# Attention's output projection in program order, its operands two tiles ahead and its input feature first in DRAM

## The chip, the core and the metric

The kernel runs on one core of a Trainium2 chip. A core has a matrix engine (TensorE, PE in the rows), three engines for element-wise work (VectorE or DVE, ScalarE or ACT, GpSimd or POOL), and SyncE (SP), which here does nothing but issue DMAs. Each engine runs its own queue of instructions in order and waits for the others by semaphores. The metric is the device time of one execution in microseconds.

## The reference

x has 2048 tokens (S) of 640 features (D); attention has 32 heads (H) of 20 features and looks back over 256 tokens; the second block is a gated MLP with 864 (FH) features a half, mixed over the tokens by a 2048 x 2048 matrix.

```
qkv = layernorm(x) @ wqkv                    # [S, 3, H, 20]
p   = softmax(q k^T / sqrt(20)), 0 <= query - key < 256
h   = x + (p @ v, heads side by side) @ wo
z   = gelu(layernorm(h) @ w_in)              # halves z1, z2 of 864
out = h + (z1 * (w_sp @ layernorm(z2) + b_sp)) @ w_out
```

## The kernel before, in words

Matrix products of float32 are made from two parts of a rounded type: a high part (a copy) and a low part (operand less high part), and three products. So each operand costs two element-wise operations, the second with two inputs; `split` and `split_o` make them.

The tokens stand in 16 tiles of 128. After the QKV stage come the attention steps: 8 groups of 4 heads, 16 key tiles each, 128 steps of `score_item` (scores and exponentials), with the row maxima of the group after it (`max_item`) made 16 steps ahead and `pv_item` (probabilities times v) 2 steps behind. Each step also issues one or two loads of 20 rows of q or k (`load_stack`, L270) for the group two further on. `pv_item` copies each 256 tokens of four heads from PSUM into a tile `ot` (L398 on ScalarE, L400 on VectorE) and stores it with one DMA (L401) into the DRAM tensor `o_d` [32 heads, 32 rows, 2048 tokens]. Of a head's 32 rows, 20 are the output, row 20 (DH) is the sum of the probabilities, the rest is unused. After the last group, `inverse_sums` loads the sums of 512 tokens (L339), takes the reciprocal on VectorE (L342) and stores it into `r_d` (L343), four times.

Then the projection with `wo`. `proj_early`, a generator that is advanced once a step through the last group, splits wo (L180, L181) and prepares tiles 0 and 1. `load_o` brings a pair of tiles from `o_d` with five DMAs (L134), features and heads on the partitions, and the inverse sums, repeated for four features, from `r_d` (L140). `norm_o` multiplies (L146), `split_o` makes the two parts (L154 or L152, L155), and `proj_o` issues 30 products (`wo_ps`, L89). The loop at L1149 goes over the tiles: it adds x (L1165), stores h to `h_d` (L1166, from ScalarE's queue), normalises over the features (`layernorm`, statistics L73 and L74 on VectorE, L75 and L76 on GpSimd, scaling L79 on VectorE), and has TensorE transpose the result two tiles later (`turn_h`, `ht_ps`, L775), ScalarE copies it out (`ho`, L650) and SP stores it (`hn_d`). Between these stand pieces of `win1_prep`: w_in in sums of blocks and their two parts, for a product by seven in place of eight blocks (`zl`, `wraw`, L644, L650), loaded at L711. The z stage begins with the products `zv` (L835).

What sets the order: from the start up to `ms.close()`, at the end of the attention loop, TensorE, VectorE, ScalarE and SP run their instructions in program order. Behind it, and on GpSimd everywhere, the scheduler of the build chooses the order, and it may move an instruction ahead into the part before, as it does with loads of x and w_in.

Of the kernel before, what the change touches and what calls it, by code (L numbers as in the profile page):

```python
# [34 lines left out]
def block_kernel(ctx, tc, x, wqk, wv, wo, w_in, wsp, bsp, w_out, out):  # L35
# [13 lines left out]
    o_d = dram.tile([H, 32, S], F32, name="o_d")  # L49
# [31 lines left out]

    def gemm(ps, n, lhs, rhs, ks):

        lh, ll = lhs
        rh, rl = rhs
        for k in range(ks):
            for a, b in ((lh, rh), (lh, rl), (ll, rh)):
                for j in range(2):
                    nc.tensor.matmul(ps[:, j, :n], a(k), b(k, j),  # L89
                                     start=(k == 0 and a is lh and b is rh),  # L90
                                     stop=(k == ks - 1 and a is ll))
# [5 lines left out]
    def open_early(pl):  # L97
        mem["t1"] = pl.tile([P, 2 * KF * D], F32R, name="t1")
        mem["m1"] = pl.tile([P, 6 * D + 4 * P], F32, name="m1")
        mem["xh"] = [pl.tile([P, D], F32, name=f"xh{i}") for i in range(2)]  # L100
        mem["ho"] = [pl.tile([P, D], F32, name=f"ho{i}") for i in range(3)]
        mem["wraw"] = pl.tile([P, 2, 2, HF], F32, name="wraw")
# [26 lines left out]
    def load_o(j):  # L129

        t = slice(2 * j * P, (2 * j + 2) * P)
        ot, rs = m1(j % 2 * 2 * D, KD, 2 * P), m1(6 * D + j % 2 * 2 * P, 2 * P)
        for k in range(KD):
            nc.sync.dma_start(ot[:, k], o_d[:, 4 * k:4 * k + 4, t])  # L134
        for i in range(2):
            ots[2 * j + i] = (ot[:, :, i * P:(i + 1) * P], rs[:, i * P:(i + 1) * P])

        def load_rs():
            base = r_d[:, t]
            nc.sync.dma_start(rs, bass.AP(tensor=base.tensor, offset=base.offset, ap=[[S, H], [0, 4], [1, 2 * P]]))  # L140

        return load_rs

    def norm_o(i, eng):
        ot, rs = ots[i]
        eng.tensor_tensor(out=ot, in0=ot, in1=rs[:, None, :].to_broadcast([P, KD, P]), op=OP.mult)  # L146

    def split_o(i, eng):
        ot, _ = ots[i]
        osp = mem["osp2"] if i % 3 == 2 else t1((2 * KD + i % 3 * 2) * D, 2, KD, P)  # L150
        if eng is nc.vector:
            eng.tensor_copy(out=osp[:, 0], in_=ot)  # L152
        else:
            nc.scalar.activation(osp[:, 0], ot, AF.Copy)  # L154
        eng.tensor_tensor(out=osp[:, 1], in0=ot, in1=osp[:, 0].bitcast(F32), op=OP.subtract)  # L155
        ots[i] = osp

# [7 lines left out]
    def proj_early():  # L165
# [10 lines left out]
        for _ in range(4):  # L176
            yield
        for k in range(KD):
            raw = raws_c.pop(f"wo{k}")
            nc.vector.tensor_copy(wo_s[:, 0, k], raw)  # L180
            nc.vector.tensor_tensor(out=wo_s[:, 1, k], in0=raw, in1=wo_s[:, 0, k].bitcast(F32), op=OP.subtract)  # L181
            if k in (1, 3):
                yield
        yield
        rs = load_o(0)
        yield
        yield
        rs()
        yield
        yield  # L190
        load_o(1)()
        yield
        for i in range(2):
            norm_o(i, nc.vector)
            split_o(i, nc.vector)
            yield


    with ExitStack() as ab:
# [132 lines left out]
        def inverse_sums(c):  # L332
            t = tmp3.tile([P, P], F32, tag="inv", bufs=2, name=f"inv{c}")

            def rows(d, step):
                return bass.AP(tensor=d.tensor, offset=d.offset, ap=[[step, H], [P, 4], [1, P]])

            yield
            nc.sync.dma_start(t, rows(o_d[:, DH, c * 512:(c + 1) * 512], 32 * S))  # L339
            yield  # L340
            yield
            nc.vector.reciprocal(out=t, in_=t)  # L342
            nc.sync.dma_start(rows(r_d[:, c * 512:(c + 1) * 512], S), t)  # L343
            yield
# [26 lines left out]
        def pv_item(u):  # L371
# [20 lines left out]
            if kb % 2:  # L392
# [4 lines left out]
                if u >= NU - 5 or j == 0 and u < NU - LEAD:  # L397
                    nc.scalar.activation(ot, src, AF.Copy)  # L398
                else:
                    nc.vector.tensor_copy(out=ot, in_=src)  # L400
                nc.sync.dma_start(o_d[4 * g:4 * g + 4, :, e:e + 256].rearrange("h d t -> (h d) t"), ot)  # L401
            if kb % 4 == 3:
                if g == 7:
                    inverse.append(inverse_sums(c))
# [176 lines left out]
        for s in range(NU + 2):  # L581
# [5 lines left out]
            for hh in range(4):  # L587
# [9 lines left out]
                if hh == 2 + s - NU and s >= NU:  # L597
                    if s == NU:
                        psB.close()
                        psW = pool(psB, "psW", space=PSUM)  # L600
                    pre_ps.append(proj_o(s - NU, psW.tile([P, 2, 512], F32, tag="wo", bufs=3, name=f"wo_ps{s - NU}")))
                if s >= 2:
                    if hh == 1:
                        pv = pv_item(s - 2)
                        next(pv, None)
                    if hh == 3:
                        next(pv, None)
            if u1 == NU:
# [12 lines left out]
        for f in inverse:  # L621
            for _ in f:
                pass


    ms.close()
# [78 lines left out]
    def win1_prep(raw):  # L705
        seven, last = win1
        src = w_in[:, :FH].rearrange("k (h c) -> k h c", h=2)
        for k in range(2):
# [5 lines left out]
            for f in right_blocks(lambda: [s[k] for s in seven], *(raw[:, b, h] for b in range(2) for h in range(2)),  # L714
                                  eng=nc.gpsimd):
# [50 lines left out]
    def turn_h(i):  # L766
        ht = mem["ho"][i % 3]
        if i < NT - 2:
# [99 lines left out]
    def z2_pair(q, i, j, k):  # L868
# [35 lines left out]
        def stat(t, h):  # L904
# [4 lines left out]
            if h:  # L909
                nc.vector.bn_aggr(out=mv[:, 0:2], in_=st)  # L910
                nc.gpsimd.tensor_scalar(out=mv[:, 2:3], in0=mv[:, 1:2], scalar1=EPS, scalar2=None, op0=OP.add)
                nc.gpsimd.tensor_tensor(out=mv[:, 3:4], in0=mv[:, 2:3], in1=half, op=OP.pow)
                nc.gpsimd.tensor_scalar(out=mv[:, 2:3], in0=mv[:, 0:1], scalar1=mv[:, 3:4], scalar2=-1.0,
                                        op0=OP.mult, op1=OP.mult)

        def norm(t):
            mv = stats[t][1]
            nc.scalar.activation(z[t], z[t], AF.Identity, bias=mv[:, 2:3], scale=mv[:, 3:4])
# [231 lines left out]
    for i in range(NT):  # L1150
        if 1 < i + 1 < NT:
            split_o(i + 1, nc.gpsimd)
        if i % 2 == 0 and i + 4 < NT:
            load_o(i // 2 + 2)()
        if i + 2 < NT:
            norm_o(i + 2, nc.vector)
        for n in (2, 3, 4) if i == 0 else (i + 4,) if i + 4 < NT else ():
            load_x2(n)
        run(i - NT)
        ps = pre_ps[i] if i < 2 else proj_o(i, acc_tile(f"wo_ps{i}"))  # L1160
        if i > 1:
            turn_h(i - 2)
        xt = hs.pop(i)
        h3 = xt.rearrange("p (a b) -> p a b", a=2)
        nc.vector.tensor_tensor(out=h3, in0=ps[:, :, :HD], in1=h3, op=OP.add)  # L1165
# [8 lines left out]
    for n in range(len(steps)):  # L1174
        run(n)
        if n < 2:
            turn_h(NT - 2 + n)
        if n == 2:
            open_d()
            w2p = win2_prep(view(fx, 4 * D + 256, FH))  # L1180
        if n > 2:
# [39 lines left out]
```

## Time and profile before

| | us |
|---|---|
| median of 3 runs | 1161.44 (1158.47 to 1166.19) |
| the profiled execution | 1165.89 |
| its span | 1163.7 |
| mean granted TensorE clock | 0.984 |

| engine | busy us | share of the span |
|---|---|---|
| TensorE | 1102.1 | 95% |
| its weight loads | 994.7 | 85% |
| VectorE | 736.8 | 63% |
| ScalarE | 553.9 | 48% |
| GpSimd | 404.8 | 35% |

The table is a mean over stages: QKV to about 248 us, attention from there to about 485, the projection to 582, then the z stage and what follows. In rows of the profile a line number is that of the kernel before, an arrow points from what is read to what is written, and "x30" counts instructions. In the kernel after the change the same code stands some ten lines lower.

### The profile page before, as it was taken

Reading aid. Unit: us, or ns where it says so; the run is one execution under the profiler, and the core shown is the slowest. Engines: PE = TensorE matmul, PEld = TensorE weight load, DVE = VectorE, ACT = ScalarE, POOL = GpSimd, SP = SyncE. Lnnn points to the kernel's source line nnn. Section 1 sums busy time; section 2 is a strip of 40 time slices with the busy share of each in tenths; the row PEclk is TensorE's granted clock in tenths of the full one; section 3 lists DMA queues with packets and bytes.
Section 4 is the critical chain, followed back from the end, with each engine's and each line's share of the span. In section 5 each row is a group of like instructions: output and inputs, shape, how many; then the busy total and the mean of one; then the engine's idle time right before and its main releaser. Section 6 shows DMA issues by size and latency. Waiting matters only on the chain.

```text
span 1163.7 us, 28646 instructions
## 1 busy us (share of the span) xinstructions
PE 1102.1 (95%) x11152; PEld 994.7 (85%) x11152; DVE 736.8 (63%) x1961; ACT 553.9 (48%) x1181; POOL 404.8 (35%) x530
## 2 busy tenths in 40 slices
PE   6999999999999999788999998999999799999998
PEld 6998886667877777588999997999999699999998
DVE  5541213788999986679858468655547874655542
ACT  4334433258998889534257566433336531222110
POOL 3124443456666667446421066000117420000000
PEclk9999999999999999889999999999999999999999
DMA  4222355545555543578736512232341454444332
GB/s 149 78 69 80 136 169 201 184 152 176 184 182 176 179 136 125 164 233 270 245 138 210 167 65 73 67 130 87 119 152 39 157 167 152 142 132 143 93 94 68
DMA packets 79800, 165.35 MB, mean 142 GB/s; under 512 B 10752, under 2 KB 43264, under 8 KB 75776
## 3 DMA queue, kind: packets, MB, share of 16 engines
q1 hardware_dynamic: 77360, 158.28, 42.0%
q10 hardware_dynamic: 2304, 5.24, 1.2%
q8 instruction: 87, 1.43, 0.5%
q14 instruction: 49, 0.40, 0.1%
HBM read 108.83 MB, written 54.66 MB: 140 GB/s over the span
## 4 chain that ended last, share of the span: by engine, by line
PE 62%; ACT 8%; issue 7%; POOL 7%; DVE 6%; DMA 6%; SPq 3%; ACTq 0%; POOLq 0%; DVEq 0%
PE g L992 21%; PE out_ps L1057 8%; ACT pt L363 5%; PE pv L386 4%; PE bank L300 3%; PE bank L361 3%; PE zx L835 2%; POOL sg L486 2%; PE zv L835 2%; PE zb L886 2%; PE zy L835 2%; PE zw L835 1%; PE wo_ps L89 1%; PE qk L467 1%; PE qk L468 1%
## 5 line engine op out<-in xcount | busy, mean ns | idle before, releaser
L363 ACT ACTIVATE pt<-bank 128x384 f32<-128x384 f32 (+2 forms) x512 | 202.5, 484 | 29.4 <-PE bank L361 22.3
L992 PE MATMUL g<-zl,aw 128*128 128x432 f32 x768 | 174.4, 363 | 8.8 <-ACT zl L650 8.3
L650 ACT ACTIVATE aw<-fx 128x512 fp32r<-128x512 f32 (+2 forms) x160 | 92.9, 595 | 187.3 <-PE g L992 122.3
L310 DVE CUSTOM_DVE_ANT_0 junk<-bank,strip 128x288 bf16<-128x288 f32 x392 | 156.2, 454 | 15.2 <-PE bank L300 13.8
L992 PEld LDWEIGHTS g<-zl,aw 128*128 128x128 f32 x768 | 145.4, 190 | 17.3 <-ACT zl L650 10.5
L992 PE MATMUL g<-ze,aw 128*128 128x432 f32 x576 | 136.2, 366 | 4.6 <-ACT aw L650 4.5
L386 PE MATMUL pv<-pt,v_sb 128*32 128x192 f32 (+3 forms) x1984 | 130.9, 326 | 10.1 <-DVE ot L400 5.0
L644 DVE TENSOR_TENSOR aw<-fx,aw 128x512 fp32r<-128x512 f32 (+2 forms) x152 | 111.9, 746 | 37.0 <-ACT aw L650 36.3
L992 PEld LDWEIGHTS g<-ze,aw 128*128 128x128 f32 x576 | 109.8, 192 | 10.3 <-ACT aw L650 5.2
L361 PE MATMUL bank<-slot 123*32 123x288 bf16 (+7 forms) x1536 | 110.0, 280 | 2.4 <-issue 1.1
L365 POOL TENSOR_SCALAR_AFFINE_SELECT pt<-pt 128x512 f32<-128x512 f32 x128 | 81.9, 640 | 70.6 <-ACT pt L363 69.3
L1057 PE MATMUL out_ps<-wout,y_sp 128*128 128x320 f32 (+1 forms) x630 | 96.2, 309 | 0.4 <-ACT y_sp L122 0.4
L886 PE MATMUL zb<-win,aw 128*128 128x432 f32 x480 | 95.3, 359 | 0.0
L1057 PEld LDWEIGHTS out_ps<-wout,y_sp 128*128 128x128 f32 (+1 forms) x630 | 94.1, 188 | 1.2 <-ACT y_sp L122 0.7
L886 PEld LDWEIGHTS zb<-win,aw 128*128 128x128 f32 x480 | 89.9, 187 | 4.7
L300 PE MATMUL bank<-slot 120*32 120x288 bf16 (+6 forms) x1280 | 92.2, 277 | 0.9 <-issue 0.8
L483 DVE TENSOR_TENSOR rest<-qk,sg 128x512 f32<-128x512 f32 x40 | 27.7, 692 | 89.5 <-ACT sg L481 89.5
L386 PEld LDWEIGHTS pv<-pt,v_sb 128*32 128x32 f32 x1984 | 61.9, 111 | 17.8 <-issue 14.3
L361 PEld LDWEIGHTS <-slot 123*32 123x32 bf16 x1728 | 60.3, 98 | 17.1 <-issue 8.3
L486 POOL TENSOR_TENSOR sg<-rest,sg 128x512 bf16<-128x512 f32 x40 | 46.5, 1164 | 75.1 <-ACT sg L485 73.2
L368 POOL TENSOR_SCALAR_AFFINE_SELECT pt<-pt 128x512 f32<-128x512 f32 x112 | 71.6, 639 | 0.0
L644 DVE TENSOR_TENSOR row<-g,row 128x432 f32<-128x432 f32 x80 | 48.2, 604 | 36.1 <-PE g L992 32.7
(192 smaller groups left out, 2221.1 us busy)
## 6 DMA issues: line engine op xcount, KB each, us to landing
slot<-qk_d SPq DMA_DIRECT2D x144, 160.0 KB
fx<-wsp_in SPq DMA_DIRECT2D x32, 512.0 KB
qk_d<-sg SPq DMA_DIRECT2D x40, 384.0 KB
fx<-hn_d SPq DMA_DIRECT2D x32, 320.0 KB
o_d<-ot SPq DMA_DIRECT2D x64, 128.0 KB
xb<-qk_d SPq DMA_DIRECT2D x48, 160.0 KB
z_d<-row SPq DMA_DIRECT2D x16, 432.0 KB
g_d<-row SPq DMA_DIRECT2D x16, 432.0 KB
```

Source lines behind the costliest of these rows:

```text
L300: nc.tensor.matmul(ps[32 * j:32 * j + 32, o:o + w], one(st, 120, 0, hh, q0, 32), k, start=True, stop=True, tile_position=(0, 32 * j))
L310: nc.vector.tensor_tensor_reduce(out=junk[:, :n], in0=ps[:, :n], in1=keep, scale=1.0, scalar=NEG, op0=OP.add, op1=OP.max, accum_out=m_cols ...
L361: nc.tensor.matmul(ps[32 * i:32 * i + 32, b + o:b + o + w], one(st, 123, 1, hh, k0, 32), q, start=True, stop=True, tile_position=(0, 32 * i))
L363: nc.scalar.activation(pt[:, hh, :n], ps[:, :n], AF.Exp, scale=SCALE)
L365: nc.gpsimd.affine_select(out=pt[:, :, :P], in_=pt[:, :, :P], pattern=[[0, 4], [1, P]], base=0, channel_multiplier=-1, compare_op=OP.is_ge ...
L386: nc.tensor.matmul(ps[32 * hh:32 * hh + 32, a - 512 * c:b - 512 * c], v_sb[:, kb, v0:v0 + 32], pt[:, hh, a - kb * P:b - kb * P], start=fir ...
L644: (eng or nc.vector).tensor_tensor(out=out, in0=a, in1=b, op=op)
L650: nc.scalar.activation(out, a, AF.Copy)
L835: nc.tensor.matmul(ps, a[x], b[:, y], start=start and m + x + y == 0, stop=stop and m == n - 1 and x == 1, skip_group_check=True)
L886: nc.tensor.matmul(b[0][:, :HF], a[t][:, x, kk], win2[0][:, y, kk, h * HF:(h + 1) * HF], start=kk + x + y == 0, stop=kk == KD - 1 and x == 1)
L992: nc.tensor.matmul(ps, w[m][:, x, k], zc[k][m][:, y], start=start and k + x + y == 0, stop=stop and k == 3 and x == 1, skip_group_check=True)
L1057: nc.tensor.matmul(ps[j][:, :HD], src[:w, a, k, :], e1["wout"][:w, b, k, j * HD:(j + 1) * HD], start=(k == 0 and a + b == 0), stop=(k == K ...
```

## The change

- `o_d` becomes [32 rows, 32 heads, tokens]. The store of `ot` writes it with an address pattern whose outer count is the 4 heads, and one load brings a pair of tiles (L145 after). The rows of wo are put in the order that goes with it. The load of the repeated inverse sums has the repetition by 4 outermost.
- VectorE makes all multiplications, low parts and sums of blocks of w_in in this stage; GpSimd keeps three small operations of the statistics a tile. ScalarE does the scaling of the normalisation (`scaled`, L90 after) in VectorE's place.
- A tile's multiplication and split are issued two tiles ahead of its projection, in place of one.
- The inverse sums are made in five pieces (256, 256 and three of 512 tokens) with buffers of their own.
- Program order lasts to step 2 of the z stage, on four engines. h is stored from SP's queue, no longer from ScalarE's.
- The split of wo goes one block a step and starts one step earlier; ScalarE makes the last copy of `ot` only, VectorE the three before it.

```diff
-    o_d = dram.tile([H, 32, S], F32, name="o_d")
+    o_d = dram.tile([32, H, S], F32, name="o_d")
...
+    def scaled(dst, src, mv):
+        nc.scalar.activation(dst, src, AF.Identity, bias=mv[:, 2:3], scale=mv[:, 3:4])
...
-        for k in range(KD):
-            nc.sync.dma_start(ot[:, k], o_d[:, 4 * k:4 * k + 4, t])
+        base = o_d[:, :, t]
+        nc.sync.dma_start(ot, bass.AP(tensor=base.tensor, offset=base.offset, ap=[[S, P], [P * S, KD], [1, 2 * P]]))
...
-            nc.sync.dma_start(rs, bass.AP(tensor=base.tensor, offset=base.offset, ap=[[S, H], [0, 4], [1, 2 * P]]))
+            nc.sync.dma_start(rs, bass.AP(tensor=base.tensor, offset=base.offset, ap=[[0, 4], [S, H], [1, 2 * P]]))
...
-        eng.tensor_tensor(out=ot, in0=ot, in1=rs[:, None, :].to_broadcast([P, KD, P]), op=OP.mult)
+        nc.vector.tensor_tensor(out=ot, in0=ot, in1=rs[:, None, :].to_broadcast([P, KD, P]), op=OP.mult)
...
-                if u >= NU - 5 or j == 0 and u < NU - LEAD:
+                if u >= NU - 2 or j == 0 and u < NU - LEAD:
                     nc.scalar.activation(ot, src, AF.Copy)
                 else:
                     nc.vector.tensor_copy(out=ot, in_=src)
-                nc.sync.dma_start(o_d[4 * g:4 * g + 4, :, e:e + 256].rearrange("h d t -> (h d) t"), ot)
-            if kb % 4 == 3:
-                if g == 7:
-                    inverse.append(inverse_sums(c))
+                base = o_d[:, 4 * g:4 * g + 4, e:e + 256]
+                nc.sync.dma_start(bass.AP(tensor=base.tensor, offset=base.offset,
+                                          ap=[[S, 4], [H * S, 32], [1, 256]]), ot)
+            if g == 7 and (kb % 4 == 3 or kb == 1):
+                n = 256 if kb < 4 else 512
+                inverse.append(inverse_sums((kb + 1) * P - n, n))
...
-            for f in right_blocks(lambda: [s[k] for s in seven], *(raw[:, b, h] for b in range(2) for h in range(2)),
-                                  eng=nc.gpsimd):
+            for f in right_blocks(lambda: [s[k] for s in seven], *(raw[:, b, h] for b in range(2) for h in range(2))):
...
-    for i in range(NT):
-        if 1 < i + 1 < NT:
-            split_o(i + 1, nc.gpsimd)
-        if i % 2 == 0 and i + 4 < NT:
-            load_o(i // 2 + 2)()
-        if i + 2 < NT:
-            norm_o(i + 2, nc.vector)
-        for n in (2, 3, 4) if i == 0 else (i + 4,) if i + 4 < NT else ():
-            load_x2(n)
-        run(i - NT)
-        ps = pre_ps[i] if i < 2 else proj_o(i, acc_tile(f"wo_ps{i}"))
-        if i > 1:
-            turn_h(i - 2)
-        xt = hs.pop(i)
-        h3 = xt.rearrange("p (a b) -> p a b", a=2)
-        nc.vector.tensor_tensor(out=h3, in0=ps[:, :, :HD], in1=h3, op=OP.add)
-        nc.scalar.dma_start(h_d[i], xt)
-        layernorm(hn(i), xt, D, f"c{i}")
-        next(w1, None)
-        if i % 2:
+    for i in range(1, NT + 1):
+        if i < NT:
+            for f in inverse:
+                next(f, None)
+                if i == 2:
+                    next(f, None)
+        if i == 1:
+            split_o(2)()
+        if 1 < i < NT:
+            pre_ps.append(proj_o(i, acc_tile(f"wo_ps{i}")))
+        if i > 1:
+            add_h(i - 1)
+        if i + 2 < NT:
+            norm_o(i + 2)
+            lo = split_o(i + 2)
+        if i == 1:
+            add_h(0)
+        if i < NT:
+            run(i - NT)
+        bn_h(i - 1)
+        if i + 2 < NT:
+            lo()
+        if i == 1:
+            load_o(2)()
+        if i % 2 and i < NT - 5:
+            load_o(i // 2 + 3)()
+        for n in (2, 3, 4) if i == 1 else (i + 3,) if i + 3 < NT else ():
+            load_x2(n)
+        next(w1, None)
+        scaled(hn(i - 1), hs.pop(i - 1), stat_h.pop(i - 1)[1])
+        if i > 1:
+            turn_h(i - 2)
+        if i % 3 == 1:
             next(w1, None)
```

`add_h` adds x and issues the store of h, `bn_h` makes the statistics, and `run` the pieces of the z stage's preparation.

What the diff does to the queues is seen in their order. First TensorE around tiles 6 to 8 of the projection. Before:

```order
L89 MATMUL wo_ps_10335<-t_9342 128x320 x13
L775 MATMUL ht_ps_10302<-ident,m_9343 128x128 x5
L89 MATMUL wo_ps_10335<-t_9342 128x320 x17
L775 MATMUL ht_ps_10366<-ident,m_9343 128x128 x5
L89 MATMUL wo_ps_10390<-t_9342 128x320 x30
L89 MATMUL wo_ps_10450<-t_9342,osp_10018 128x320 x28
L775 MATMUL ht_ps_10421<-ident,m_9343 128x128 x5
L89 MATMUL wo_ps_10450<-t_9342,osp_10018 128x320 x2
```

After:

```order
L784 MATMUL ht_ps_10290<-ident,m_9343 128x128 x5
L99 MATMUL wo_ps_10298<-t_9342 128x320 x30
L784 MATMUL ht_ps_10348<-ident,m_9343 128x128 x5
L99 MATMUL wo_ps_10356<-t_9342 128x320 x30
L784 MATMUL ht_ps_10405<-ident,m_9343 128x128 x5
L99 MATMUL wo_ps_10415<-t_9342,osp_10008 128x320 x30
L784 MATMUL ht_ps_10461<-ident,m_9343 128x128 x5
```

Before, the scheduler put a tile's transposes (`ht_ps`) inside a projection (`wo_ps`) or left them out between two; now one set stands behind each projection.

Next VectorE where attention ends and wo is split; `ot_1_0` and its like are the copies of the last group's output, `CAST` and the subtraction behind it split one block of wo. Before:

```order
L180 CAST t_9342<-m_9343 128x640
L181 TENSOR_TENSOR t_9342<-m_9343,t_9342 128x640
L180 CAST t_9342<-m_9343 128x640
L181 TENSOR_TENSOR t_9342<-m_9343,t_9342 128x640
L400 COPY ot_1_0_9624<-pv_1_9481 128x256
L180 CAST t_9342<-wraw 128x640
L181 TENSOR_TENSOR t_9342<-wraw,t_9342 128x640
L342 RECIPROCAL inv_9524<-inv_9524 128x128
L400 COPY ot_1_1_9699<-pv_1_9481 128x256
L400 COPY ot_2_0_9767<-pv_2_9656 128x256
```

After:

```order
L412 COPY ot_0_1_9522<-pv_0_9401 128x256
L191 CAST t_9342<-m_9343 128x640
L192 TENSOR_TENSOR t_9342<-m_9343,t_9342 128x640
L191 CAST t_9342<-m_9343 128x640
L192 TENSOR_TENSOR t_9342<-m_9343,t_9342 128x640
L412 COPY ot_1_0_9625<-pv_1_9483 128x256
L191 CAST t_9342<-m_9343 128x640
L192 TENSOR_TENSOR t_9342<-m_9343,t_9342 128x640
L354 RECIPROCAL inv_9347<-inv_9347 128x64
L191 CAST t_9342<-wraw 128x640
L192 TENSOR_TENSOR t_9342<-wraw,t_9342 128x640
L412 COPY ot_1_1_9697<-pv_1_9483 128x256
```

The splits now stand between the copies, and the reciprocals, each of 256 tokens, ahead of the copy `ot_1_1`.

Third, ScalarE and SP at the start of the projection's loop after the change; `zl` from `wraw` is the first high part of a block of w_in, L90 the scaling, `L721` the load of w_in. ScalarE:

```order
L165 ACTIVATE osp_10008<-m_9343 128x640
L165 ACTIVATE t_9342<-m_9343 128x640
L90 ACTIVATE m_9343<-xh_9344,mvc_10043 128x640
L165 ACTIVATE t_9342<-m_9343 128x640
L660 ACTIVATE zl_10012<-wraw 128x432
L90 ACTIVATE m_9343<-xh_9345,mvc_10097 128x640
L660 ACTIVATE ho_9348<-ht_ps_10108 128x640
```

SP:

```order
L1159 DMA h_d<-xh_9344 128x640
L145 DMA m_9343<-o_d 128x5x256
L151 DMA m_9343<-r_d 128x1x256
L145 DMA m_9343<-o_d 128x5x256
L151 DMA m_9343<-r_d 128x1x256
L138 DMA xh_10005<-x_in 128x640
L138 DMA xh_10006<-x_in 128x640
L138 DMA xh_10007<-x_in 128x640
L721 DMA wraw<-w_in_in 128x864 x2
```

On ScalarE the piece of w_in stands ahead of the scaling of tile 1 (`xh_9345`), and on SP its load stands behind the first store of h and the loads of two pairs of tiles and three tiles of x; before the change, the scaling was VectorE's and did not stand behind a piece of w_in on ScalarE.

More of the change, by code (lines that the diff above doesn't have):

```diff
@@ L100, in open_early @@
         mem["xh"] = [pl.tile([P, D], F32, name=f"xh{i}") for i in range(2)]
+        mem["inv"] = [pl.tile([P, P], F32, name=f"inv{i}") for i in range(2)]
         mem["ho"] = [pl.tile([P, D], F32, name=f"ho{i}") for i in range(3)]
@@ L175, in proj_early @@
             load_x2(i)
-        for _ in range(4):
+        for _ in range(3):
             yield
@@ L342, in inverse_sums @@
             nc.vector.reciprocal(out=t, in_=t)
-            nc.sync.dma_start(rows(r_d[:, c * 512:(c + 1) * 512], S), t)
+            nc.sync.dma_start(rows(r_d[:, t0:t0 + n], S), t)
             yield
@@ L607, in block_kernel @@
                         next(pv, None)
+                if hh == 2 + s - NU and s >= NU:
+                    if s == NU:
+                        psB.close()
+                        psW = pool(psB, "psW", space=PSUM)
+                    pre_ps.append(proj_o(s - NU, psW.tile([P, 2, 512], F32, tag="wo", bufs=3, name=f"wo_ps{s - NU}")))
             if u1 == NU:
```

85 lines of the change are left out of this document (45 added, 40 removed).

## The prediction

> **What bounds the kernel now.** I read the busy time by stretches first, then the chain of waits, then TensorE's own timeline and waits around the projection. The stretches (columns: length, then busy time of TensorE, its weight loads, VectorE, ScalarE and GpSimd, the granted TensorE clock, the DMA share and GB/s) show which stage is not full:
>
> ```profile
> core 0: us, PE busy (x) PEld busy (x) DVE busy (x) ACT busy (x) POOL busy (x), PEclk, DMA share, GB/s
> 466.00:488.00 22.00, 13.73 (x261) 9.60 (x258) 10.70 (x16) 12.78 (x36) 11.37 (x17) 0.83 0.57 182
> 488.00:582.00 94.00, 85.28 (x562) 82.67 (x562) 79.78 (x131) 30.70 (x54) 49.25 (x52) 0.93 0.73 238
> 582.00:740.00 158.00, 153.27 (x769) 144.84 (x768) 109.38 (x185) 95.01 (x172) 50.75 (x51) 0.98 0.35 120
> ```
>
> TensorE is nearly full, but in the projection (488 to 582) it is busy 85 of 94 us at a clock of 0.93, and in the seam before it 14 of 22 us at 0.83. The chain of waits at the end of that stage shows its pace when nothing is late:
>
> ```profile
> 567.85 4.39 PE wo_ps L89 x30
> 572.25 0.55 PE ht_ps L775 x5
> 572.79 4.40 PE wo_ps L89 x30
> 577.20 0.55 PE ht_ps L775 x5
> ```
>
> A tile takes 4.40 us of projection and 0.55 us of transposes: 4.95 us. TensorE's timeline (start, length, work, in brackets the idle time and who ended it) shows where it was slower:
>
> ```profile
> 471.19 1.08 PE L386 MATMUL pv<-pt,v_sb 128*32 128x256 f32 x8 [5.00 <-DVE ot L400]
> 487.69 5.93 PE L89 MATMUL wo_ps<-t 128*128 128x320 f32 x30 [2.22 <-DVE t L152]
> 509.98 0.74 PE L775 MATMUL ht_ps<-ident,m 128*128 128x128 f32 x5 [1.95 <-DVE m L79]
> 512.27 7.16 PE L89 MATMUL wo_ps<-t 128*128 128x320 f32 x30 [1.55 <-DVE xh L1165]
> 538.23 5.88 PE L89 MATMUL wo_ps<-t,osp 128*128 128x320 f32 x28 [2.92 <-DVE mvc L74]
> 577.50 4.64 PE L89 MATMUL wo_ps<-t 128*128 128x320 f32 x30
> 582.44 1.43 PE L835 MATMUL zv<-zl,aw 128*128 128x432 f32 x6
> 514.00:517.00 3.00, 3.00 (x13) 3.00 (x13) 2.97 (x5) 2.10 (x4) 2.41 (x4) 0.50 0.97 332
> ```
>
> After each wait the next projection is longer too: 5.93, 7.16 and 5.88 us (the last with 28 of 30 products) against 4.64, because the granted clock falls (0.50 in the stretch after the waits at 510 and 512). VectorE ended all these waits.
>
> From the first projection at 487.69 to the first product of the z stage at 582.44 are 94.75 us, and sixteen projections with fifteen transposes at full pace are 16 x 4.40 + 15 x 0.55 = 78.65 (this stretch holds 14 of the transposes now, 15 with the change). So at most 16.1 us can be saved there, 16.6 with the transposes that leave the z stage.
>
> **The change part by part.** *TensorE's order.* Before, transposes stand inside a projection and wait for a normalised tile; now projection and transposes alternate, the normalised tile being due one tile earlier than its transposes. Nothing is added on TensorE. If no operand is late this gives the 16.6 us.
>
> *VectorE and GpSimd.* These rows show durations next to each other and alone:
>
> ```profile
> 488.32 1.55 DVE L146 TENSOR_TENSOR m<-m 128x640 f32<-128x640 f32 x2
> 546.76 2.92 DVE L146 TENSOR_TENSOR m<-m 128x640 f32<-128x640 f32 x2
> 546.74 2.26 POOL L155 TENSOR_TENSOR osp<-m,osp 128x640 fp32r<-128x640 f32 x1
> L146 DVE TENSOR_TENSOR m<-m 128x640 f32<-128x640 f32 x16 | 15.4, 995 | 6.6 <-DMA m<-o_d 3.5 <-DMA hn_d<-ho 1.7 <-DMA r_d<-inv 1.4
> L79 DVE TENSOR_SCALAR m<-xh,mvc 128x640 f32<-128x640 f32 x15 | 12.4, 824 | 5.3 <-POOL mvc L76 5.3
> 487.58 0.82 DVE L155 TENSOR_TENSOR t<-m,t 128x640 fp32r<-128x640 f32 x1
> L644 DVE TENSOR_TENSOR wraw<-wraw 128x432 f32<-128x432 f32 x4 | 2.4, 598 | 0.0
> L154 ACT ACTIVATE t<-m 128x640 fp32r<-128x640 f32 x9 | 6.6, 730 | 11.5 <-DMA m<-o_d 8.8 <-PE wo_ps L89 2.7
> ```
>
> Alone, two of the multiplications by the inverse sums take 1.55 us; beside GpSimd's subtraction they take 2.92. VectorE now gets fourteen subtractions of GpSimd's (14 x 0.82 = 11.5) and eight pieces of win1 (8 x 0.60 = 4.8), loses the scaling to ScalarE (12.4) and the slow-down of the multiplications (16 x (0.995 - 0.775) = 3.5). From 79.8 us busy that makes about 80.2; the other two-input operations that shared time with GpSimd should give back a few us more, and I take 77: 4.8 us a tile, hidden behind TensorE's 4.95 with little to spare. ScalarE's 30.7 us grow by 15 scalings at about the 0.73 us of its other 128x640 operation to 42 of 80: hidden. If the cover is gone, an overrun of VectorE goes straight into the pace (a rival below).
>
> *The seam.* Before, TensorE waits 5.0 us for a copy that stands on VectorE behind four pairs of splits of wo. With the change the first split stands ahead of one copy, where it waits for wo to land, and the first inverse sums stand ahead of another. I expect two waits of about 2 and 3 us in place of the one, so no gain; bounds for the first projection are 3 us earlier (neither waits) and 3 us later (both are as long as the one now).
>
> *A new wait.* In the new program order ScalarE's second piece of win1 stands ahead of the scaling of tile 1, and it waits for a load of w_in that SP issues behind the first store of h, two pairs of attention output and three tiles of x. In the trace that load left SP at 478.57, ahead of them all. Its row, that of the first addition to h, and the sizes:
>
> ```profile
> 478.57 0.44 SPq L711 DMA_DIRECT2D wraw<-w_in_in  x1
> 494.24 0.75 DVE L1165 TENSOR_TENSOR xh<-wo_ps,xh 128x640 f32<-128x640 f32 x1
> h_d<-xh ACTq DMA_DIRECT2D x15, 320.0 KB
> m<-o_d SPq DMA_DIRECT2D x35, 128.0 KB
> m<-r_d SPq DMA_DIRECT2D x8, 128.0 KB
> xh<-x_in SPq DMA_DIRECT2D x11, 320.0 KB
> wraw<-w_in_in SPq DMA_DIRECT2D x3, 432.0 KB
> ```
>
> One h_d, two pairs of 5 x 128 + 128 KB, three x and two blocks of w_in (one into fx, and the one waited for) are 3680 KB or 3.8 MB, at the 332 GB/s of the full stretch above some 11 us. The store of h waits for the first addition, which came 6.6 us after the first projection and now stands behind another multiplication, a split and the pieces of the inverse sums: about 10 us, an estimate. So w_in lands near 22 us, ScalarE's piece and the scaling follow, and the transposes of tile 1 can start near 24; TensorE, after four projections of 4.64 and one set of transposes, would be there at 19. I take 4.9 us of waiting (0 if SP gets through sooner, 8 if the loads go at the stage's mean of 238 GB/s) and 1.8 us for the clock after it (0 to 2.5, from 7.16 against 4.64).
>
> *The loads and stores.* One load for a pair in place of five saves issues on SP, which bounds nothing. The stores of the attention output now go to an address pattern whose outer count is 4 instead of 128. How many of the 16 engines a transfer uses can be read from its small closing packets. An isolated store (432 to 436 us) and a stretch with nothing but the 20-row loads of q and k (182 to 184 us):
>
> ```profile
> DMA packets 146, 0.16 MB, mean 39 GB/s; under 512 B 16, under 2 KB 144, under 8 KB 144
> q1 hardware_dynamic: 144, 0.13, 9.8%
> DMA packets 93, 0.51 MB, mean 254 GB/s; under 512 B 31, under 2 KB 31, under 8 KB 31
> ```
>
> The store has 128 rows and 16 closing packets; the loads have 62 rows of 8 KB with 31 closing packets, ten for twenty rows. So the shape sets the engines, and an outer count of 4 may well mean four. The store takes 0.098 x 16 x 4 = 6.3 us of engine time, 0.39 on each of sixteen, 1.6 on each of four: later by 1.2 us, of which in the middle of attention nobody takes notice as long as those four engines keep up. I put it at 0 there, from the slack of half a group that the loads have, and keep the upper end for the rival. *The Trainium skill, "DMA: Bandwidth & Descriptors", section "Why a DMA increments its semaphore by 16 and not by 1", says that a transfer runs on the largest number of engines up to 16 that divides the outermost count of both patterns, and always on the lowest-numbered ones. By that rule the loads' ten agree with the trace, and the stores would be on four that all loads use too; by it the second rival has the better chance, and the sum would be its time.*
>
> **The sum.** 1165.9 us (the profiled execution: span 1163.7 and 2.2 around it) - 16.6 + 4.9 + 1.8 = 1156.0. The profiled execution lies 4.5 us above the median of the runs shown (1161.44), so the forecast is 1151.5. With the bounds together, not all at one end, 1145 to 1158.
>
> **The rivals.** *The new wait is not there.* w_in is in time, for example because the loads pass SP early; all 16.6 us come: 1161.4 - 16.6 = 1144.8, 1144 with a somewhat earlier seam. For it speaks that DMA is at 0.73 in this stage; against it, that SP's order puts everything ahead of that load.
>
> *Four engines carry the stores and fill up (slower).* Price from these rows:
>
> ```profile
> L401 SPq DMA_DIRECT2D o_d<-ot x64: 319/410/1570, 257.9 to 497.8; - x64
> 181.00:184.00 3.00, 3.00 (x15) 2.41 (x14) 0.69 (x1) 1.23 (x2) 0.67 (x2) 1.00 0.62 257
> q1 hardware_dynamic: 2296, 5.48, 57.5%
> slot<-qk_d SPq DMA_DIRECT2D x23, 160.0 KB
> ```
>
> 64 stores in 239.9 us make 30.4 us for a group of eight. A load of 160 KB keeps its ten engines for 0.64 us at 257 GB/s; in the stretch 310 to 340 all 26 loads (these 23 and 3 into another buffer) and 8 stores have 57.5% of 16 x 30 us = 276, so less 8 x 6.3 a load costs 226 / 26 / 10 = 0.87. With 24 loads and 8 stores at 1.57, four engines need 27.9 us a group at the first price and 33.4 at the second, against 30.4. Above 0.74 us a load they decide: at 0.87 each of six groups is 3.0 us longer, 18 us, and the five stores on the way to the inverse sums add 1.2 each: 1151.5 + 24 = 1175. For it speak the closing packets; against it, that a long packet in a mixed stretch may only overlap another.
>
> *VectorE becomes the bound.* In program order it can't fill a wait with later work, and its 4.8 us a tile are uneven, since preparation of win1 and of the z stage falls on a few tiles. If a tile costs 0.6 us more than TensorE's pace, 16 x 0.6 = 9.6 are given back: 1161.
>
> **How the numbers follow.** A measurement of this kernel can tell about 1% from no change: below 1149.8 is faster, above 1173.1 slower. Chances: forecast 0.42 (four tenths of it below 1149.8), no new wait 0.26 (nearly all faster), four engines 0.22 (two thirds slower), VectorE 0.10 (half slower, as an uneven pace may cost more than worked out). That gives faster 0.44, same 0.36, slower 0.20. The likeliest case's own range is 1145 to 1158; to leave out no more than two in ten the range reaches to 1141 on the side of the first rival and 1172 into the second.
>
> **What would show it.** Right: projections of 4.4 with transposes of 0.55 between them without a break from the fourth tile on, the first product of the z stage 84 to 88 us after the first projection, GpSimd nearly empty there, VectorE's multiplications at 0.75 to 0.8 us, and one gap ahead of the transposes of tile 1 that ScalarE or the load of w_in ended. Wrong: attention longer than from 257.9 to 497.8 by its stores, SP waiting on transfers of m_d or q and k, 32 rows for one closing packet in an isolated store (four engines), or many short gaps that VectorE ended. The stages after the z stage should not move.

## The result and the profile after

The changed kernel takes 1179.31 us (1177.71 to 1183.03, 4 runs) against 1159.95 for the kernel before on the same chip: a ratio of 1.0161, 95% interval 1.0131 to 1.0192. It is slower by 19 us where 10 us less were forecast. The profiled execution is 1183.0 us with a span of 1181.3.

The same stretches as before the change (length, busy time of TensorE, weight loads, VectorE, ScalarE and GpSimd, clock, DMA share, GB/s), and with them the stretch from the first projection to the first product of the z stage:

```profile
466.00:488.00 22.00, 19.24 (x481) 13.28 (x477) 13.96 (x34) 19.91 (x55) 18.56 (x26) 1.00 0.48 151
488.00:582.00 94.00, 75.60 (x603) 72.23 (x591) 57.66 (x103) 36.23 (x67) 25.06 (x44) 0.85 0.68 225
582.00:740.00 158.00, 154.76 (x826) 147.64 (x825) 113.90 (x201) 98.27 (x176) 52.42 (x57) 1.00 0.43 149
506.40:601.20 94.80, 85.00 (x574) 83.52 (x572) 66.10 (x125) 40.64 (x65) 24.45 (x45) 0.92 0.73 245
```

The first row is still full of attention: everything has moved later. TensorE's timeline shows by how much, and what became of the projection:

```profile
505.57 0.87 PE L398 MATMUL pv<-pt,v_sb 128*32 128x192 f32 x8 [6.34 <-DVE ot L412]
506.37 7.08 PE L99 MATMUL wo_ps<-t 128*128 128x320 f32 x30
537.00 1.33 PE L784 MATMUL ht_ps<-ident,m 128*128 128x128 f32 x5 [9.15 <-ACT m L90]
537.98 6.67 PE L99 MATMUL wo_ps<-t 128*128 128x320 f32 x30
549.89 4.64 PE L99 MATMUL wo_ps<-t 128*128 128x320 f32 x30
554.84 4.65 PE L99 MATMUL wo_ps<-t 128*128 128x320 f32 x30
601.21 1.43 PE L844 MATMUL zv<-zl,aw 128*128 128x432 f32 x6
605.23 1.45 PE L844 MATMUL zx<-zl,aw 128*128 128x432 f32 x6 [2.58 <-ACT ho L660]
```

The first projection starts at 506.37 in place of 487.69, 18.7 us later. From there to the first product of the z stage (`zv`) it takes 94.84 us, as before (94.75): the pace between is the predicted 4.95 us a tile (549.89 to 554.84), but a slow first projection (7.08 us), one wait of 9.15 us and the slow projection behind it (6.67 us) eat the gain. Behind it 1181.3 - 601.2 = 580.1 us remain, before 581.3. So the loss is all ahead of the projection. What SP and TensorE waited for between 250 and 480 us (total, times, longest), SP and TensorE before, then SP and TensorE after, and the stores of `ot` after:

```profile
SPq L327 <- DMA m_d<-m: 19.5, 14, 3.4
...
PE bank L361 <- DMA slot<-m_d: 0.7, 1, 0.7
...
SPq L338 <- DMA m_d<-m: 40.6, 15, 5.1
...
PE bank L373 <- DMA slot<-m_d: 12.2, 4, 4.7
PE bank L373 <- DMA xb<-m_d: 3.9, 2, 2.2
...
L414 SPq DMA_DIRECT2D o_d<-ot x64: 512/553/630, 260.5 to 514.4; - x64
```

SP waits twice as long for its store of the row maxima (`m_d`) before it loads them again, and TensorE, which waited 0.7 us for those loads before, waits 16.1 us for them. The stores stretch over 253.9 us (before 239.9), 32.2 us for a group of eight in place of 30.4. The first store starts 2.6 us later than before (260.5 for 257.9), behind a stage that the change leaves alone, and the runs below have it anywhere from 257.9 to 262.4; so some 16 of the 18.7 us arise between it and the first projection. An isolated store, 463 to 467 us (busy share of the engines in 40 slices of 0.1 us, then the packets):

```profile
DMA  0000000023131223228223232000000000000000
DMA packets 133, 0.15 MB, mean 37 GB/s; under 512 B 4, under 2 KB 132, under 8 KB 132
```

and the slices of the one before the change, whose packets the prediction shows (432 to 436 us):

```profile
DMA  0000000000003999500000000000000000200600
```

It now has 4 closing packets (those under 512 B) to its 128 rows, where it had 16, and lasts 1.8 us at a fifth to a quarter of the engines, where it took 0.5 at nearly all.

### The profile page after: what moved, and what is told of

It is laid out like the page before. It is cut to its first block, busy times and chain, and to the rows that moved or that the text cites. A ratio compares the mean times of both kernels' runs of the same rounds, so it can differ in the third digit from the quotient of the medians.

```text
span 1181.3 us, 28599 instructions
## 1 busy us (share of the span) xinstructions
PE 1106.7 (94%) x11152; PEld 998.9 (85%) x11152; DVE 732.2 (62%) x1970; ACT 566.5 (48%) x1194; POOL 380.8 (32%) x524
## 4 chain that ended last, share of the span: by engine, by line
PE 40%; DVE 6%; DMA 5%; POOL 4%; ACT 3%; issue 2%; SPq 0%; DVEq 0%; POOLq 0%; ACTq 0%
PE g L996 20%; PE out_ps L1061 8%; PE zx L844 2%; PE zv L844 2%; PE zb L895 2%; PE zy L844 2%; PE zw L844 1%; DMA m<-r_d 1%; PE wo_ps L99 1%; DVE zl L654 1%; PE yt_ps L1050 1%; POOL row L654 1%; ACT row L90 1%; DVE aw L654 1%; DMA h_d<-xh 1%
## 5 line engine op out<-in xcount | busy, mean ns | idle before, releaser
L660 ACT ACTIVATE aw<-fx 128x512 fp32r<-128x512 f32 (+3 forms) x160 | 93.0, 595 | 172.3 <-PE g L996 113.7
L398 PE MATMUL pv<-pt,v_sb 128*32 128x192 f32 (+3 forms) x1984 | 134.9, 332 | 15.5 <-DVE ot L412 10.1
L654 DVE TENSOR_TENSOR aw<-fx,aw 128x512 fp32r<-128x512 f32 (+3 forms) x152 | 108.5, 724 | 35.2 <-ACT aw L660 34.3
L373 PE MATMUL bank<-slot 123*32 123x288 bf16 (+8 forms) x1536 | 111.6, 281 | 0.5 <-ACT pt L375 0.2
L377 POOL TENSOR_SCALAR_AFFINE_SELECT pt<-pt 128x512 f32<-128x512 f32 x128 | 82.6, 645 | 81.0 <-ACT pt L375 78.8
L311 PE MATMUL bank<-slot 120*32 120x288 bf16 (+5 forms) x1280 | 92.5, 277 | 0.2
L373 PEld LDWEIGHTS <-slot 123*32 123x32 bf16 x1728 | 62.9, 100 | 25.9 <-issue 17.3
L380 POOL TENSOR_SCALAR_AFFINE_SELECT pt<-pt 128x512 f32<-128x512 f32 x112 | 73.9, 660 | 0.0
```

What stands on the lines that cost most here:

```text
L311: nc.tensor.matmul(ps[32 * j:32 * j + 32, o:o + w], one(st, 120, 0, hh, q0, 32), k, start=True, stop=True, tile_position=(0, 32 * j))
L373: nc.tensor.matmul(ps[32 * i:32 * i + 32, b + o:b + o + w], one(st, 123, 1, hh, k0, 32), q, start=True, stop=True, tile_position=(0, 32 * i))
L377: nc.gpsimd.affine_select(out=pt[:, :, :P], in_=pt[:, :, :P], pattern=[[0, 4], [1, P]], base=0, channel_multiplier=-1, compare_op=OP.is_ge ...
L398: nc.tensor.matmul(ps[32 * hh:32 * hh + 32, a - 512 * c:b - 512 * c], v_sb[:, kb, v0:v0 + 32], pt[:, hh, a - kb * P:b - kb * P], start=fir ...
L654: (eng or nc.vector).tensor_tensor(out=out, in0=a, in1=b, op=op)
L660: nc.scalar.activation(out, a, AF.Copy)
```

## The experiments

Theory A, the prediction's second rival: an outer count of 4 puts the store on four engines, which the loads of q and k use as well; the transfers of `m_d` queue behind both. Rivals: B, the new addresses make the stores slow; C, the store's longer issue on SP (0.55 us for 0.41); D, the program order around the end of attention.

**1. Only the pattern (e1_outer4).** In the kernel before:

```diff
-                nc.sync.dma_start(o_d[4 * g:4 * g + 4, :, e:e + 256].rearrange("h d t -> (h d) t"), ot)
+                base = o_d[4 * g:4 * g + 4, :, e:e + 256]
+                nc.sync.dma_start(bass.AP(tensor=base.tensor, offset=base.offset,
+                                          ap=[[32 * S, 4], [S, 32], [1, 256]]), ot)
```

> The kernel before, with one edit: the store of ot is written with an address pattern of outer count 4 (4 x 32 x 256). Addresses, bytes and the number of transfers are those of before. Theory A (an outer count of 4 puts the store on four engines, which the loads of q and k use too, and the transfers of m_d queue behind both): SP waits for m_d for some 40 us in attention as in the changed kernel (20 before), the 64 stores stretch over 252 us or more (240 before), 1160 + 12 to 16 = 1172 to 1176 us. Theory B (the new addresses, a head's rows 256 KB apart, make the store slow): nothing moves, 1158 to 1163. Theory C (only the store's longer issue on SP counts, 0.55 for 0.41 us): 64 x 0.14 = 9 us at most, 1160 to 1169, and SP's waits for m_d stay near 20 us.

1161.90 us, ratio 0.9992 (0.9972 to 1.0012). It tested nothing: with these strides the two outer counts are one count of 128 rows, and so the build issued it. An isolated store of this run, 433 to 437 us, has 16 closing packets:

```profile
DMA packets 146, 0.16 MB, mean 39 GB/s; under 512 B 16, under 2 KB 144, under 8 KB 144
```

**2. The layout of before in the changed kernel (e2_layout).** `o_d` is [heads, rows, tokens] again, with all that hangs on it:

```diff
-    o_d = dram.tile([32, H, S], F32, name="o_d")
+    o_d = dram.tile([H, 32, S], F32, name="o_d")
...
-                                          ap=[[S, 4], [H * S, 32], [1, 256]]), ot)
+                nc.sync.dma_start(o_d[4 * g:4 * g + 4, :, e:e + 256].rearrange("h d t -> (h d) t"), ot)
...
-            nc.sync.dma_start(rs, bass.AP(tensor=base.tensor, offset=base.offset, ap=[[0, 4], [S, H], [1, 2 * P]]))
+            nc.sync.dma_start(rs, bass.AP(tensor=base.tensor, offset=base.offset, ap=[[S, H], [0, 4], [1, 2 * P]]))
```

> The changed kernel with the DRAM layout of before: stores of 128 rows, five loads a pair, inverse sums repeated inside, rows of wo as before. Program order, split of work and two tiles ahead stay. Theory A: SP's waits for m_d fall from 40.6 to about 20 us, the 64 stores to about 240 us, the first projection comes 13 to 16 us earlier, the wait ahead of the transposes of tile 1 shrinks by about 2 us: 1159 to 1165. Rival (the slow-down is of the order, VectorE behind waits in the last steps): the first projection gains at most 5 us, 1172 to 1178.

1166.18 us, ratio 1.0032 (1.0011 to 1.0053): of the 19 us of loss some 4 are left. SP's waits for m_d, the stores, and TensorE at the projection:

```profile
SPq L338 <- DMA m_d<-m: 15.6, 13, 2.4
...
L413 SPq DMA_DIRECT2D o_d<-ot x64: 319/410/1201, 258.9 to 494.8; - x64
...
487.05 6.76 PE L99 MATMUL wo_ps<-t 128*128 128x320 f32 x30
515.74 1.33 PE L782 MATMUL ht_ps<-ident,m 128*128 128x128 f32 x5 [7.51 <-ACT m L90]
```

The first projection comes 19.3 us earlier, where it was before the change: D falls. But what is left of the change gains nothing either, which the next runs are about.

**3. The load of w_in ahead of the loop (e3_win),** and **4. with the layout of before (e4_both):**

```diff
     w1 = win1_prep(mem["wraw"])
+    next(w1)
...
-        next(w1, None)
+        if i > 1:
+            next(w1, None)
         scaled(hn(i - 1), hs.pop(i - 1), stat_h.pop(i - 1)[1])
```

> The changed kernel with the first load of w_in issued ahead of the loop over tiles, so ahead of the first store of h, the loads of two pairs and three tiles of x. Theory: the wait of 9.15 us ahead of the transposes of tile 1 was for this load alone; it goes, with the 2 us of low clock behind it: 1167 to 1171. Rival: the attention output of tile 4 is as late (VectorE waited for its inverse sums until 527), so that a wait of 2 to 5 us stays and the gain is 4 to 8 us: 1171 to 1175.

> Both edits together, the layout of before and the early load of w_in. If the two costs are the whole loss and independent: 1179 - 16 - 10 = 1150 to 1155, 0.5 to 0.9% below before, with 80 to 84 us from the first projection to the first product of the z stage. If they share a cause (both are DMA in the same stage), less than the sum: 1156 to 1162.

1178.60 us, ratio 1.0134 (1.0090 to 1.0178), and 1164.98 us, ratio 1.0014 (0.9988 to 1.0039). Both gain less than expected. TensorE in the first, then VectorE and TensorE in the second:

```profile
527.35 1.33 PE L784 MATMUL ht_ps<-ident,m 128*128 128x128 f32 x5 [4.49 <-ACT m L90]
...
503.67 0.82 DVE L157 TENSOR_TENSOR m<-m 128x640 f32<-128x640 f32 x1 [8.04 <-DMA m<-o_d]
508.33 1.33 PE L782 MATMUL ht_ps<-ident,m 128*128 128x128 f32 x5 [4.78 <-ACT m L90]
```

The wait ahead of tile 1's transposes only falls from 9.15 to 4.49 us, and with the layout of before from 7.51 to 4.78: now VectorE's multiplication of tile 4 waits at the head of VectorE's queue, 7.77 us for its inverse sums in run 3 and 8.04 for its load in run 4, and tile 1's statistics stand behind it. The rival of run 3 had that wait, but not so small a gain.

**5. The layout alone, in the kernel before (e5_layout_alone):** the first edit of run 2 the other way, with the five loads, the scheduler and all else as before.

> The kernel before with the DRAM layout of the change alone: o_d feature first, stores of 4 x 32 x 256, rows of wo to go with it, the repetition of the inverse sums outermost; five loads a pair, scheduler's order and everything else as before. (In the first run of this kind the pattern of outer count 4 had been merged to 128 rows, with 16 closing packets, so it tested nothing; here the strides can't be merged.) Theory A (four engines): an isolated store has 4 closing packets and takes about 1.8 us, SP's waits for m_d rise from 20 to some 40 us, the first projection comes 11 to 16 us later: 1172 to 1180. Rival (the loss comes from program order in the last steps): 1160 to 1165.

1181.83 us, ratio 1.0154 (1.0125 to 1.0183), SP's waits for m_d, the stores, and the packets of one finished store and part of the next (461 to 465 us):

```profile
SPq L327 <- DMA m_d<-m: 42.1, 15, 4.5
...
L402 SPq DMA_DIRECT2D o_d<-ot x64: 517/552/978, 262.4 to 516.1; - x64
...
DMA packets 186, 0.20 MB, mean 50 GB/s; under 512 B 4, under 2 KB 185, under 8 KB 185
```

The layout alone, its stores and its loads together, makes the whole loss; run 12 takes the stores by themselves.

**6 and 9. More issues on SP (e6_sp_issue, e9_sp_24).** The kernel of run 2 with a small extra store behind each store of ot, and behind 24 of the 64:

```diff
+                if (2 * c + j) % 3 == 0:          # run 9 only
+                    nc.sync.dma_start(e_d[8 * g + 2 * c + j], ot[:16, :64])
```

> The changed kernel with the layout of before, and one small extra store (16 rows of 256 B, to a scratch tensor) behind each store of ot, so that SP issues 64 more DMAs of some 0.3 us (more issue time than the 0.14 us by which the store of the change took longer), while the data on each engine hardly grows. Theory A: as without them, 1164 to 1170, SP's waits for m_d below 25 us. Rival (the store's longer issue on SP made the loss): 1175 or more, with loads of q and k issued later.

> As the run with 64 extra small stores, but with 24 of them: at the 0.43 us median that one took on SP that is 10 us more for SP in attention, about what the longer issue of the change's stores costs (64 x 0.14 = 9 us). Theory A (the waits for m_d behind the four engines made the loss, the issue time little of it): within 4 us of the run with the layout of before alone, 1164 to 1170. Rival (SP has no spare time, so that 10 us of issue cost as much): 1173 to 1178.

1182.57 us, ratio 1.0172 (1.0134 to 1.0210), and 1170.31 us, ratio 1.0052 (1.0014 to 1.0090). SP's and TensorE's waits for m_d and the small stores in the first, SP's waits in the second:

```profile
SPq L339 <- DMA m_d<-m: 13.3, 10, 3.1
...
PE bank L374 <- DMA slot<-m_d: 7.9, 4, 5.8
PE bank L374 <- DMA xb<-m_d: 5.4, 2, 2.9
...
L415 SPq DMA_DIRECT2D e_d<-ot x64: 311/427/1641, 260.5 to 510.0; - x64
...
SPq L339 <- DMA m_d<-m: 23.0, 15, 3.0
```

Run 6 went against A's expectation. 64 extra issues, 27 us at their median and more in all, cost 16 us against run 2. SP does not wait longer for m_d, but TensorE now waits 13.3 us for those loads, and none in run 2: a busy SP can bring them late too. Run 9 has the dose that fits C, 24 x 0.43 = 10 us: the first projection came at 489.7 in place of 487.05, and the intervals of runs 2 and 9 overlap. So, as an estimate, the longer issue explains some 3 of the 19 us. Whether SP's 21 us of added waiting for m_d are the rest, run 10 asks.

**7. The loads earlier (e7_early)** and **8. the last transposes too (e8_best).** On the kernel of run 4, in `proj_early` behind `norm_o(2)`, and for run 8 in the loop:

```diff
+        src = w_in[:, :FH].rearrange("k (h c) -> k h c", h=2)
+        for b in range(2):
+            nc.sync.dma_start(mem["wraw"][:, b], src[2 * b * P:(2 * b + 1) * P])
+        load_o(2)()
...
+        if i == NT:                               # run 8 only
+            turn_h(i - 2)
         scaled(hn(i - 1), hs.pop(i - 1), stat_h.pop(i - 1)[1])
-        if i > 1:
+        if 1 < i < NT:
             turn_h(i - 2)
```

The loads of x for tiles 2 to 4 stand ahead of the loop.

> The layout of before, and the loads of w_in, of the third pair of tiles and its inverse sums issued at the end of the preparation of tiles 0 and 1, x of tiles 2 to 4 ahead of the loop. Theory: what remained ahead of the transposes of tile 1 (4.8 us and about 2 us of low clock) was VectorE's multiplication of tile 4 waiting for its load, at the head of its queue: it goes, 81 to 86 us from the first projection to the first product of the z stage (91.4 with the early load of w_in alone), 1156 to 1161. Rival: the transfers only move the crowding into the last steps of attention, and the first projection comes later by what is gained: 1162 to 1167.

> The same, and the transposes of tile 14 with their copy ahead of the scaling of tile 15 on ScalarE. Theory: the 2.6 us for which the z stage's second product waited (ScalarE's copy stood behind a scaling that waits for GpSimd's statistics) go, with the low clock behind them: 3 to 4 us below the run without it, 1152 to 1158, faster than the kernel before by 0.4 to 0.9%. Rival: the z stage is held by its loads anyway: no difference.

1158.06 us, ratio 0.9968 (0.9945 to 0.9990), and 1156.28 us, ratio 0.9940 (0.9919 to 0.9962). TensorE in run 7 at the start of the z stage, then in run 8:

```profile
577.12 2.48 PE L847 MATMUL zx<-zl,aw 128*128 128x432 f32 x6 [2.58 <-ACT ho L662]
...
486.51 6.05 PE L99 MATMUL wo_ps<-t 128*128 128x320 f32 x30
497.46 4.56 PE L99 MATMUL wo_ps<-t,osp 128*128 128x320 f32 x30
502.33 4.65 PE L99 MATMUL wo_ps<-t 128*128 128x320 f32 x30
507.28 4.64 PE L99 MATMUL wo_ps<-t 128*128 128x320 f32 x30
L847 PE MATMUL zv<-zl,aw x120: 352/358/444, 569.2 to 657.7; 128*128 128x432 f32 x120
```

Now no tile waits in between, and from the first projection to the first product of the z stage it takes 82.7 us, 12 fewer than before. The wait of 2.58 us ahead of `zx` is gone in run 8: there ScalarE's copy of tile 14 no longer stands behind the scaling of tile 15, which waits for GpSimd's statistics. Run 8 beats both kernels, the one before by 0.6%. A second profile (run 11: its label says otherwise, but the kernel is that of run 8):

> The version with the layout of before, early loads and the transposes of tile 14 ahead, once more, for the spread of its profile: 1153 to 1158, the first projection near 486 to 489.

1155.38 us, one run; the first projection starts at 488.7 us.

**10. The row maxima loaded later (e10_rows_late).** In the changed kernel, stores still on four engines:

```diff
-                if hh == 3 and u1 % 8 == 1 and 1 < s <= NU - LEAD + 1:
+                if hh == 3 and u1 % 8 == 4 and 4 < s <= NU - LEAD + 4:
                     next(rows)
```

> The changed kernel with one line moved: the load of the row maxima from m_d is issued three steps later (it is needed eight steps after the store), stores still on four engines. Theory A as I now put it (SP, in order, waits for the m_d store, which queues on the four engines; what is behind it on SP comes late): SP's waits for m_d fall from 40.6 us to below 10, the first projection comes 8 to 14 us earlier, 1166 to 1172. Rival (the four engines are full in themselves, whatever SP does): the waits move to the loads of q and k, 1175 to 1180.

1188.03 us, ratio 1.0213 (1.0176 to 1.0249): slower still. SP's and TensorE's waits in the whole of attention (250 to 500 and 250 to 505 us), then the issue of one such load and when TensorE got it, in this run and in the changed kernel:

```profile
SPq L414 <- ACT pt L375: 49.8, 24, 6.5
SPq L338 <- DMA m_d<-m: 2.9, 1, 2.9
...
PE bank L373 <- DMA slot<-m_d: 16.8, 6, 5.6
PE bank L373 <- DMA xb<-m_d: 7.7, 2, 4.8
...
322.39 0.44 SPq L338 DMA_DIRECT2D xb<-m_d  x1
...
328.15 0.18 PE L373 MATMUL bank<-xb,xb 123*32 123x32 bf16 x1 [4.80 <-DMA xb<-m_d]
...
322.42 0.25 SPq L338 DMA_DIRECT2D xb<-m_d  x1
...
324.64 0.18 PE L373 MATMUL bank<-xb,xb 123*32 123x32 bf16 x1 [2.18 <-DMA xb<-m_d]
```

SP hardly waits for m_d any more, and TensorE waits longer than in the changed kernel, 24.5 us in all for 16.1. So SP's order is not what makes the loss, as I had put it for this run: taking its wait away only hands it to TensorE. The two loads shown were both issued at 322.4 us, and TensorE got the row maxima 5.8 us after the issue here and 2.2 us after it in the changed kernel. Between the store and the load of the row maxima SP had issued six loads of q and k and two stores of `ot` here, two loads and one store there. So it is the load itself that takes longer, behind more transfers; that it queues behind them on the same engines fits this, but is not shown.

**12. The engines without the addresses (e12_pad).** In the kernel before, heads 33 rows apart, so that 4 x 32 can't be merged:

```diff
-    o_d = dram.tile([H, 32, S], F32, name="o_d")
+    o_d = dram.tile([H, 33, S], F32, name="o_d")
...
+                                          ap=[[33 * S, 4], [S, 32], [1, 256]]), ot)
```

> The kernel before with heads 33 rows apart in o_d in place of 32, so that a store's address pattern of 4 heads x 32 rows can't be merged to 128 rows. Neighbouring rows lie 8 KB apart as before; bytes, transfers and the layout for the loads are those of before. If the outer count of 4 alone makes the loss (four engines): an isolated store has 4 closing packets and lasts some 1.8 us, SP waits some 40 us for m_d, 1174 to 1182. Rival (the addresses of the feature-first layout, rows of one head 256 KB apart, make it): 1158 to 1165, 16 closing packets or short stores all the same.

1177.33 us, ratio 1.0142 (1.0092 to 1.0191). SP's waits, the stores, and the packets of one finished store and part of the next:

```profile
SPq L327 <- DMA m_d<-m: 43.0, 15, 4.8
...
L402 SPq DMA_DIRECT2D o_d<-ot x64: 517/557/576, 257.9 to 510.1; - x64
...
DMA packets 202, 0.22 MB, mean 55 GB/s; under 512 B 4, under 2 KB 201, under 8 KB 201
```

The rows lie 8 KB apart as before, and the loss is there: B falls. What counts is the outer count of the pattern, and with it, by the closing packets, the number of engines.

**The runs together.** TensorE's wait for loads of m_d in attention is 0 us in run 2, 2.9 in run 9, 13.3 in run 6, 14.7 in run 12, 15.3 in run 5, 16.1 in the changed kernel and 24.5 in run 10. The medians lie 4, 7, 20, 14, 19, 19 and 24 us above that of the kernel before on the same chip. For no other transfer does TensorE wait there in any of them. So the loss goes with the late arrival of the row maxima, whether slow stores make it or a busy SP; run 6 has more to it than this wait.

## Why the prediction was wrong, by its steps

**TensorE's order, right.** 4.95 us a tile, and with all operands in time (run 8) 82.7 us from the first projection to the z stage, 12.0 below before, where 16.1 was the bound.

**VectorE, right in direction.** GpSimd keeps only the small operations (24.5 us busy of 94.8, before 49 of 94), a multiplication takes 0.82 us (0.775 forecast, 0.995 before). VectorE is busy 66 us, not the 77 of the prediction, so that rival had little to stand on.

**The seam, right without the stores.** Run 2 has its first projection within 0.7 us of before, though with three waits for VectorE's copies (2.3, 2.0 and 4.3 us) where two of about 2 and 3 us were expected.

**The new wait, right in place and mis-sized.** It stood ahead of tile 1's transposes, behind ScalarE's piece of w_in, and measured 9.15 us for 4.9. ScalarE's row, then SP's for the first store of h and the load of w_in:

```profile
535.58 0.56 ACT L660 ACTIVATE zl<-wraw 128x432 fp32r<-128x432 f32 x1 [6.12 <-DMA wraw<-w_in_in]
```

```profile
519.09 0.42 SPq L1159 DMA_DIRECT2D h_d<-xh  x1
...
525.09 1.31 SPq L721 DMA_DIRECT2D wraw<-w_in_in  x2
```

w_in came 29 us after the first projection, not 22. SP issued the load, by the row above, 18.7 us after it. The store of h, estimated at 10 us, left at 12.7, and from there to w_in's landing it took 16.5 us, not 11. And it was not alone: with it out of the way the load of tile 4 was as good as next (runs 3 and 4). This step asked only which operand would come last, not which would come next to last.

**The stores, the step that failed.** "I put it at 0 there, from the slack of half a group that the loads have": it was 13 to 19 us (runs 2, 5 and 12). The price of the store was right (1.6 us forecast, 1.8 measured on four engines), and so was the place. What was wrong was the cover. The loads of q and k do have that slack, TensorE waited for none of them; the row maxima do not have it, and TensorE waited 16.1 us for their loads. The prediction's own last part named m_d as a sign, but its sum gave it nothing. The rival's 1175 us came near, but partly by luck: its 33.4 us a group at the upper price lie above the 32.2 measured, and it priced full engines and the loads of q and k, not the row maxima. *The Trainium skill, "DMA: Bandwidth & Descriptors", section "Why a DMA increments its semaphore by 16 and not by 1", had the count of engines from the pattern; here 4 closing packets agree with it (runs 5 and 12 and the changed kernel), 16 where the pattern merges (run 1).* Which of the engines those are, no view here shows. I gave that rival 0.22.

**Left out altogether.** The z stage's second product waited 2.58 us, and then the clock was low (0.66, by this stretch of run 4), because the copy of tile 14 stood behind a scaling on ScalarE. The prediction had only counted TensorE's transposes there, and took their move for a gain.

```profile
579.00:584.00 5.00, 5.00 (x21) 4.64 (x21) 2.70 (x6) 1.74 (x5) 0.00 (x0) 0.66 0.32 110
```

Together: the order and the split of work are worth having (run 8), but as they stand, with the loads behind one another on SP, they gave nothing (run 2), and the layout took 13 us or more by itself (runs 5 and 12).

## What to carry to other kernels

A new DRAM layout is first a question of the outer count of each address pattern: count the closing packets of an isolated transfer in the profile, and don't take comfort in the mean share of all sixteen engines. What came late here was not the transfer that got slower but a small one with less slack; look for the DMA that the engine which sets the pace begins to wait for, and not only for what the issuing queue waits for. When a queue in program order waits for one load, move everything the next instructions need with it, or the second load takes the place of the first.

## What the runs showed of the hardware

A store of 128 rows of 1 KB lasts 0.5 us with 16 closing packets and 1.8 us with 4; it takes SP 0.41 us to issue the first and 0.55 the second. Patterns of 4 x 32 whose strides join are issued as 128 rows (run 1), 33 rows apart they are not (run 12). And with DMA at a mean share of 0.53 in attention before and 0.48 in run 12 (250 to 486 us), one such pattern cost this kernel 1.4% (run 12).
